# Second inversion ended in load 1 with its transpositions apart, first weight in whole rows, copies of the mixing and gram products ahead of conversion

## The chip, the core and the metric

The kernel runs on one core of a Trainium2 chip. A core has engines that run side by side, each through its own queue in order: TensorE (PE, matrix products, with PEld for its weight loads), VectorE (DVE), ScalarE (ACT), GpSimd (POOL), and SyncE (SP), which here only issues transfers (DMAs) between memory and the core. The metric is device time in microseconds from the launch's begin to its end; lower is better.

## The reference

For each of 4 batches and 8 heads (head size 48, 768 steps), a delta rule runs over the steps:

```python
k_n = k / (np.linalg.norm(k, axis=-1, keepdims=True) + 1e-06)
for t in range(S):
    y[:, :, t] = einsum(q[:, :, t], state)
    v_old = einsum(state, k_n[:, :, t])
    state = state + beta[t] * outer(k_n[:, :, t], v[:, :, t] - v_old)
```

The heads' outputs are put side by side (`x`, 768 x 384 for each batch), and a second block follows:

```python
mixed = real(fft(fft(x, axis=1), axis=2))
u = x + mixed
un = (u - mean(u)) / sqrt(var(u) + 1e-06)
out = u + maximum(un @ w_ch1, 0) @ w_ch2
```

`w_ch1` is 384 x 1536 and `w_ch2` 1536 x 384. Both arrive as 64-bit floats; all else is 32-bit.

## The kernel before, in words

**Blocks.** The recurrence is computed in loads of 128 steps: 6 loads to a batch, 24 in all, `g` is the load's number. In a load, chunks of 64 steps are turned into products: a gram matrix of the keys (`pre_a`, which copies the turned keys KT, L321, and the gram G, L380 and L386, and its masked half GU, L396), the inverse of a triangular matrix built from it, and then steps that carry the state S from chunk to chunk (`step`, with U at L721 and S at L740) and give the load's outputs (`outputs`, L763 and L773).

**Inversions.** Four loads share one inversion (`invert16`, `invert`), which runs on DVE. `invert16(1)` serves loads 4 to 7. It is a generator of 46 steps: a transposition in, 12 small operations on the norms and a scaling, then 15 pairs of a product (L518) and a sum (L521), and two transpositions of 128 x 1024 elements at the end: G (L524) and A (L526), both reading M. `pre_m16(g)` uses them: its first step copies G to Z on ACT (L609), its second makes PE's product of Z with GU, copies it to ND (L618) and copies A to MT (L625); three more products follow (L646, L648, L650), then the values are scaled (L630) and multiplied.

**Conversion.** `weight(0)` and `weight(1)` load the two weights in 12 pieces each of 384 KB and build 32-bit floats from the 64-bit words. A piece goes through ACT (L277, L282, L283) and DVE (L278, L294, L298, L300 and, one or two pieces later, the final product L290), and the next piece's load is issued behind it (L255). `convert(1)` and `advance(conv, n)` move this generator by half a piece at a time; a conversion step in the texts is two such halves. The first weight's pieces are 128 columns of all three row blocks, so a load has runs of 1 KB; the second's are one row block of all columns, runs of 3 KB. The first weight's temporary buffer takes the place of M of the inversion.

**Mixing and the two products.** `fourier(b)` gives one block of 128 rows at a time: PE's product with `dtab`, a copy Q on ACT (L874), and six operations on DVE (L883 to L891). `mlp(b)` normalizes (L912), turns (PE transpositions, copies unT at L923), makes the first product over 12 column blocks (`first_of`, its result copied as hT, L933) and the second (`second_of`). PE's results lie in pools of two buffers each: `pair`, `one` (also for the turned keys and the mixing) and `post` (the two products of the second block and its transpositions). A PE product waits until the copy that reads a buffer has been made.

**Order.** The order of PE, DVE, ACT and POOL is written out by hand in the program text, by advancing generators (`with tc.manual_schedule`). Two places differ. SP's order is always a planner's. And in loads 6 and 7 only PE's order is by hand: there a planner with its own estimates orders the other engines, and may also place their instructions among the last ones of the part before.

Loads 0 to 5 (the first batch) are a loop of their own: in each, `nm` is `pre_m16` of the next load and `n2` of the one after, `late` the outputs of the load before, c0 and c1 the two chunk steps, and `fill(n)` issues n steps of the second inversion, or, where it has ended, of the folds before the mixing. Then `fourier(0)` begins, and a loop over the 12 column blocks of the first product (`for fc in range(KF)`) issues for each block: the product and its copy hT (`side`); one conversion step; in blocks 1, 3, 6 and 9 one row block of the mixing (`f`); and one piece of `rest`, the keys of loads 9 to 11 (k1, k2, k3), the last steps of `pre_m16(7)` and the queries of load 6. The third inversion (`invert16(2)`) is issued after it, in loads 6 and 7.

Of the kernel before, what the change touches and what calls it, by code (L numbers as in the profile page):

```python
# [64 lines left out]
def kernel(  # L65
# [13 lines left out]
    DFF = moe_w_ch1.shape[1]  # L79
# [3 lines left out]
    KD = DM // 128  # L83
# [129 lines left out]
    w1 = const.tile([128, KD, DFF], F32, name="w1")  # L213
# [10 lines left out]
    def weight(last):  # L224

        if moe_w_ch1.dtype == F32:
            if last:
                nc.sync.dma_start(out=w2, in_=moe_w_ch2.rearrange("(c p) m -> p c m", p=128))  # L230
            else:
                nc.sync.dma_start(out=w1, in_=moe_w_ch1.rearrange("(c p) f -> p c f", p=128))
            return
        w1v = moe_w_ch1.bitcast(I32).rearrange("(c p) (f two) -> p c f two", p=128, two=2)
        w2v = moe_w_ch2.bitcast(I32).rearrange("(c p) (m two) -> p c m two", p=128, two=2)
        n = DM
        flat = "p e t m -> p (e t m)"
        if last:
            pieces = [(w2v[:, i:i + 1], w2[:, i:i + 1]) for i in range(KF)]

            E, O3 = spare.pop()
            ring = E.rearrange(flat).bitcast(I32).rearrange("p (i m two) -> p i m two", m=n, two=2)
            tmp = O3.rearrange(flat).rearrange("p (i e m) -> p i e m", e=2, m=n)
            tmp = [tmp[:, i] for i in range(3)]
            deep = 3
        else:
            pieces = [(w1v[:, :, i:i + 128], w1[:, :, i:i + 128]) for i in range(0, DFF, 128)]
            ring = wk.tile([128, 4, n, 2], I32, tag="big", bufs=2, name="w64")
            tmp = None
            deep = 4  # L250

        def stage(i):
            if i < len(pieces):
                src = pieces[i][0]
                nc.sync.dma_start(  # L255
                    out=ring[:, i % deep].rearrange("p (c f) two -> p c f two",
                                                    c=src.shape[1]), in_=src)

        for i in range(deep):
            stage(i)  # L260
        yield
        if tmp is None:
            tmp = [wk.tile([128, 2, n], F32, tag="M", name="wtmp0"),
                   wk.tile([128, 2, n], F32, tag="unT", bufs=2, name="wtmp1")]

        def of(i):
            t = tmp[i % len(tmp)]
            return ring[:, i % deep, :, 0], ring[:, i % deep, :, 1], t[:, 0], t[:, 1].bitcast(I32)


        lag = len(tmp) - 1
        for i in range(len(pieces) + lag):
            if i < len(pieces):
                lo, hi, man, num = of(i)


                nc.scalar.activation(man, lo.bitcast(U32), ACT.Copy, scale=2.0 ** -52, bias=1.0)  # L277
                nc.vector.tensor_scalar(num, hi, 0xFFFFF, None, op0=ALU.bitwise_and)  # L278
            if 0 < i <= len(pieces):

                num0 = of(i - 1)[3]
                nc.scalar.activation(num0, num0, ACT.Relu, scale=-1.0, bias=edges[:, 0:1])  # L282
                nc.scalar.activation(num0, num0, ACT.Relu, scale=-2.0 ** 23,  # L283
                                     bias=edges[:, 1:2])
            yield
            if i >= lag:
                _, _, man0, num0 = of(i - lag)
                dst = pieces[i - lag][1]
                c = dst.shape[1]
                nc.vector.tensor_tensor(dst, man0.rearrange("p (c f) -> p c f", c=c),  # L290
                                        num0.bitcast(F32).rearrange("p (c f) -> p c f", c=c),
                                        op=ALU.mult)
            if i < len(pieces):
                nc.vector.scalar_tensor_tensor(man, num, 2.0 ** -20, man, op0=ALU.mult,  # L294
                                               op1=ALU.add)

                man = man.bitcast(I32)
                nc.vector.scalar_tensor_tensor(man, hi, -2 ** 31, man, op0=ALU.bitwise_and,  # L298
                                               op1=ALU.bitwise_or)
                nc.vector.tensor_scalar(num, hi, 20, 0x7FF, op0=ALU.logical_shift_right,  # L300
                                        op1=ALU.bitwise_and)
                stage(i + deep)
            yield
# [7 lines left out]
    KTs, Gs, GXs, rounds, pre, xs = {}, {}, {}, {}, {}, {}  # L311
# [147 lines left out]
    def invert16(r):  # L459

        G = Gs.pop(r)
# [12 lines left out]
        A, M, Ad, Md = whole(A2), whole(M2), blocks(A2), blocks(M2)  # L474
# [38 lines left out]
        for j in range(V16 - 1):  # L513
            n = V16 - 1 - j
# [7 lines left out]
                                    op=ALU.add)  # L522
            yield
        nc.vector.transpose(G.rearrange("p m s -> p s m"), M.rearrange("p t s -> p s t"))  # L524
        yield
        nc.vector.transpose(A.rearrange("p m t -> p t m"), M)  # L526
        rounds[r] = (A, G, nT)
        yield

    LQs = {}  # L530
# [432 lines left out]
    def advance(gen, n=1):  # L963
        for _ in range(n):
            if next(gen, "end") == "end":
                return False
        return True

    def drain(gen):
        for _ in gen:  # L970
            pass
# [121 lines left out]
    with tc.manual_schedule(engines=engines):  # L1093
# [65 lines left out]
        def convert(n):  # L1159
            advance(conv, n)  # L1160

        def fill(n):

            while n > 0 and advance(inv1):
                n -= 1
            while n > 0 and advance(fd):
                n -= 1

        keys = [pre_a(g) for g in range(2 * RL, 3 * RL)]
        for g in range(NL - 1):  # L1170
            c0, c1 = step(g, 0), step(g, 1)
            nm, n2 = ms[g + 1], ms[g + 2]
            load_k(g + 2)
            load_v(g + 2)
            if g == 0:
                advance(c0)
                fill(4)
                advance(nm)
                advance(n2)
                advance(c1)  # L1180
                fill(4)
                advance(nm)
                advance(n2)
                advance(c1)
                fill(4)
                advance(nm)
                advance(n2)
                drain(nm)
                advance(n2)
                drain(qs[1])  # L1190
                advance(qs[2])
                advance(ms[3])
            else:
                advance(c0)
                fill(4)
                if g == 2:
                    drain(inv1)
                    advance(n2)
                if g > 1:
                    convert(1)  # L1200
                advance(nm)
                advance(late)
                advance(c0)
                fill(4)
                advance(n2)
                drain(late)
                if g == 4:
                    fold = folds(0)
                    fd = part(fold, 8)
                    advance(keys[0])  # L1210
                advance(nm)
                advance(c1)
                fill(3)
                if g > 1 and g != 4:
                    convert(2)
                drain(nm)
                advance(n2)
                advance(c1)
                if g == 4:
                    convert(2)  # L1220
                    advance(n2)
                    drain(qs[g + 1])
                    convert(1)
                else:
                    fill(3)
                    if g > 1:
                        convert(1)
                    advance(n2)
                    if g > 1:
                        convert(g - 1)  # L1230
                    drain(qs[g + 1])
                if g + 2 < NL:
                    advance(qs[g + 2])
                if g > 1 and g < 4:
                    advance(ms[g + 3])
            late = outputs(g)
            if g == 1:
                nc.sync.dma_start(out=evt, in_=cn["even"].ap())
                nc.sync.dma_start(out=odt, in_=cn["odd"].ap())
                nc.sync.dma_start(out=dtab, in_=cn["dtab"].ap())  # L1240
            if g == 2:
                for i in range(2 * RL, 2 * RL + 3):
                    load_c(i)
                load_q(NL)
                load_q(NL + 1)
# [44 lines left out]
        rest = [k1, ms[7], k1, ms[7], k2, ms[7], k2, k3, nq, k3]  # L1290
        for fc in range(KF):
            advance(side)
            advance(conv, 2)
            if fc in (1, 3, 6, 9):
                advance(f)
            if fc < len(rest):
                advance(rest[fc])
        drain(f)
        for m in ms[6:] + keys[1:]:
            drain(m)  # L1300
# [54 lines left out]
```

## Time and profile before

Four runs took 748.22, 752.25, 752.93 and 752.98 us: median 752.59.

| | us |
|---|---|
| median of the runs | 752.59 |
| the profiled execution | 748.22 |
| its span, first to last instruction | 746.4 |
| PE busy in the span | 690.0 |
| DVE busy | 377.5 |
| ACT busy | 264.4 |
| the two weights' products on PE (ph and po) | 208.5 and 204.7 |

Times in all lists are microseconds from the span's start. L12 is line 12 of the kernel. In a row of a timeline stand the start, the duration, the engine, the line, the operation, what it writes and reads (`out<-in`), the size, how many instructions were merged, and in brackets how long the engine stood idle before and what ended that. The granted clock is the share of TensorE's full clock that the chip let it have. `E` and `O` in conversion rows are buffers in which the second weight is converted.

In the chain of work that ended last, PE holds 74% of the span, DVE 16%, ACT 5%. The first batch's loads take the time from 40 to 113 us, the mixing begins there, the loop over column blocks runs from 131 to 167 us, and loads 6 and 7 with the third inversion from there to 203 us.

### The profile page before, as it was taken

The numbers are of one execution on the slowest core, as the hardware profiler recorded it, in microseconds if no ns is written. First come the engines' busy times: TensorE is split into PE (matmuls) and PEld (weight loads), VectorE is DVE, ScalarE is ACT, GpSimd is POOL, SyncE is SP. The second block draws the span as 40 slices with busy tenths as digits, with TensorE's granted clock in tenths as the row PEclk, the third lists the DMA queues.
The fourth block names the chain that finished last, engine by engine and source line by source line (L and its number), as shares of the span: only waits on it lengthen the run. The fifth ranks groups of instructions, "written<-read, shape, count | busy, mean of one in ns | idle before, by whom it ended". The sixth has DMA issues, their size and how long they took to land.

```text
span 746.4 us, 23081 instructions
## 1 busy us (share of the span) xinstructions
PE 690.0 (92%) x10176; PEld 529.5 (71%) x10176; DVE 377.5 (51%) x957; ACT 264.4 (35%) x644; POOL 78.7 (11%) x138
## 2 busy tenths in 40 slices
PE   7877878797999978999999999999999999999998
PEld 4676767675767656878768778878677688777684
DVE  5867877689812797261497228188312241600000
ACT  5544763787424222224322333133223121311120
POOL 8000000110000012021010220030112000200000
PEclk8799999989999998999999999999999999999999
DMA  9942452053113221002222211011210000000000
GB/s 153 220 74 41 118 117 85 12 138 102 35 40 69 56 47 20 10 11 57 50 45 49 45 40 28 1 33 34 44 33 14 12 12 1 22 1 21 11 11 21
DMA packets 111863, 36.10 MB, mean 48 GB/s; under 512 B 101873, under 2 KB 109842, under 8 KB 111762
## 3 DMA queue, kind: packets, MB, share of 16 engines
q1 hardware_dynamic: 109938, 33.86, 21.2%
q8 instruction: 80, 1.31, 0.7%
q0 software_dynamic: 640, 0.43, 0.4%
q10 hardware_dynamic: 1184, 0.33, 0.3%
q14 instruction: 21, 0.17, 0.1%
HBM read 29.88 MB, written 4.72 MB: 46 GB/s over the span
## 4 chain that ended last, share of the span: by engine, by line
PE 74%; DVE 16%; ACT 5%; issue 2%; DMA 1%; POOL 0%; DVEq 0%; ACTq 0%; SPq 0%
PE po L110 24%; PE ph L110 22%; PE one L110 15%; PE pair L110 9%; PE one L113 2%; DVE M L451 1%; DVE tmp L447 1%; PE ptr L113 1%; DVE w L290 1%; PE unread L1106 1%; ACT wtmp L283 1%; DMA C<-in_k_dram 1%; ACT wtmp L282 1%; DVE M L521 1%; PE pf L110 1%
## 5 line engine op out<-in xcount | busy, mean ns | idle before, releaser
L110 PE MATMUL ph<-unT,w 128*128 128x256 f32 x864 | 208.5, 393 | 1.1 <-ACT unT L923 0.6
L110 PE MATMUL po<-w,hT 128*128 128x384 f32 x576 | 204.7, 494 | 0.0
L110 PEld LDWEIGHTS ph<-unT,w 128*128 128x128 f32 x864 | 162.8, 194 | 26.2 <-ACT hT L933 0.9
L110 PEld LDWEIGHTS po<-w,hT 128*128 128x128 f32 x576 | 103.5, 190 | 56.3
L933 ACT ACTIVATE hT<-ph 128x256 f32<-128x256 f32 x144 | 55.2, 383 | 146.7 <-PE ph L110 145.9
L946 DVE TENSOR_TENSOR x<-x,po 128x384 f32<-128x384 f32 x24 | 13.2, 551 | 107.0 <-PE po L110 107.0
L740 DVE TENSOR_TENSOR S<-S,pair 128x192 f32<-128x192 f32 x40 | 14.0, 350 | 72.2 <-PE pair L110 72.1
L110 PEld LDWEIGHTS one<-V,MT 64*64 64x64 f32 x768 | 29.0, 136 | 20.6 <-issue 8.8
L883 DVE TENSOR_TENSOR x<-x,one 128x193 f32<-128x193 f32 x24 | 8.5, 354 | 68.7 <-ACT Q L874 68.7
L110 PE MATMUL one<-V,MT 64*64 64x48 f32 x768 | 34.2, 223 | 4.7 <-DVE V L699 2.7
L451 DVE TENSOR_TENSOR M<-M,tmp 128x31 f32<-128x31 f32 (+15 forms) x93 | 34.5, 371 | 3.2
L447 DVE TENSOR_TENSOR tmp<-A,M 128x31 f32<-128x31 f32 (+15 forms) x93 | 34.1, 366 | 2.5
L699 DVE TENSOR_TENSOR V<-V,pair 128x192 f32<-128x192 f32 x33 | 11.5, 349 | 38.2 <-PE pair L110 31.4
L110 PEld LDWEIGHTS one<-dtab,F 97*128 97x128 f32 (+1 forms) x192 | 25.1, 191 | 7.3 <-ACT KT L321 2.2
L895 POOL TENSOR_SCALAR rstd<-mv 128x1 f32<-128x1 f32 x24 | 6.4, 266 | 223.2 <-DVE mv L891 223.2
L110 PE MATMUL one<-MT,ND 64*64 64x64 f32 x768 | 27.7, 219 | 0.9 <-ACT MT L648 0.7
L321 ACT ACTIVATE QT<-one 128x512 f32<-128x512 f32 x24 | 14.2, 594 | 39.5 <-PE one L113 39.4
L110 PE MATMUL one<-dtab,F 97*128 97x97 f32 (+1 forms) x192 | 26.0, 275 | 1.8 <-ACT KT L321 1.8
L110 PEld LDWEIGHTS pair<-S,KT 48*64 48x64 f32 x528 | 10.7, 133 | 22.6 <-issue 11.0
L110 PEld LDWEIGHTS one<-MT,ND 64*64 64x64 f32 x768 | 25.1, 135 | 2.3 <-ACT MT L648 0.8
L567 POOL TENSOR_TENSOR MT<-A,pack 128x512 f32<-128x512 f32 x12 | 12.7, 1055 | 130.8 <-PE one L110 65.2
L110 PEld LDWEIGHTS pair<-U,K 64*64 64x64 f32 x704 | 15.3, 133 | 15.2 <-issue 13.0
(178 smaller groups left out, 1012.1 us busy)
## 6 DMA issues: line engine op xcount, KB each, us to landing
w<-in_moe_w_ch_dram SPq DMA_DIRECT2D x12, 384.0 KB, 5.8
E<-in_moe_w_ch_dram SPq DMA_DIRECT2D x12, 384.0 KB, 3.3
out_dram<-x SPq DMA_DIRECT2D x24, 192.0 KB, 1.9
K<-in_k_dram SPq DMA_DIRECT2D x92, 48.0 KB, 2.5
V<-in_v_dram SPq DMA_DIRECT2D x92, 48.0 KB, 2.3
C<-in_k_dram SPq DMA_DIRECT2D x18, 192.0 KB, 9.2
Q<-in_q_dram SPq DMA_DIRECT2D x18, 192.0 KB, 3.4
w<-in_q_dram SPq DMA_DIRECT2D x6, 192.0 KB, 8.2
```

The source lines that it names most:

```text
L110: nc.tensor.matmul(o, lhsT=lhsT, rhs=rhs, start=start, stop=stop, skip_group_check=True)
L113: nc.tensor.matmul(o, lhsT=src, rhs=ident[0:src.shape[0], 0:src.shape[0]], is_transpose=True, start=start, stop=True, skip_group_check=True)
L282: nc.scalar.activation(num0, num0, ACT.Relu, scale=-1.0, bias=edges[:, 0:1])
L321: nc.scalar.activation(dst.rearrange("p h j t -> p (h j t)"), pt, ACT.Copy)
L447: nc.vector.tensor_tensor(t, A[:, j + 1:W, j:j + 1].broadcast_to([128, n, j + 1]), M[:, j:j + 1, 0:j + 1].broadcast_to([128, n, j + 1]), o ...
L451: nc.vector.tensor_tensor(M[:, j + 1:W, 0:j + 1], M[:, j + 1:W, 0:j + 1], t, op=ALU.add)
L567: nc.gpsimd.tensor_tensor(MT, MTd[:, m8, None, :].broadcast_to([128, 8, 2, W]), m_blk[:, None, :, None].broadcast_to([128, 8, 2, W]), op=A ...
L699: nc.vector.tensor_tensor(R4, R4, pw[:, :, 0:2 * D].rearrange("p a (j e) -> p a j e", e=D), op=ALU.subtract)
L740: nc.vector.tensor_tensor(s1v, s0.rearrange("p h j e -> p h (j e)"), pk, op=ALU.add)
L883: nc.vector.tensor_tensor(near, near, pb[:, 0, 0:MH + 1], op=ALU.add)
L933: nc.scalar.activation(hT[:, fc, :], ph, ACT.Relu)
L946: nc.vector.tensor_tensor(x[:, T, :], x[:, T, :], po, op=ALU.add)
```

## The change

In `weight`, the first weight's pieces become one row block by 384 columns. In `invert16`, the entry in `rounds` is made between the two last transpositions, so that `pre_m16` may be issued between them. In the loop over loads 0 to 4 the fills of loads 0 and 1 grow to 5, 5, 5 and 5, 5, 4, 1; in load 2 the first step of `n2` comes right after c0, without a fill, and the rest of the inversion, now only A's transposition, after c0's second half, with the first conversion half behind it. In the loop over column blocks the conversion step moves behind the mixing and `rest`.

```diff
@@ weight
-            pieces = [(w1v[:, :, i:i + 128], w1[:, :, i:i + 128]) for i in range(0, DFF, 128)]
+            pieces = [(w1v[:, c:c + 1, i:i + n], w1[:, c:c + 1, i:i + n])
+                      for i in range(0, DFF, n) for c in range(KD)]
@@ invert16
         nc.vector.transpose(G.rearrange("p m s -> p s m"), M.rearrange("p t s -> p s t"))
+        rounds[r] = (A, G, nT)
         yield
         nc.vector.transpose(A.rearrange("p m t -> p t m"), M)
-        rounds[r] = (A, G, nT)
         yield
@@ loads 0 to 4, g == 0
-                fill(4)
+                fill(5)
...
@@ loads 0 to 4, g > 0
                 advance(c0)
-                fill(4)
                 if g == 2:
-                    drain(inv1)
                     advance(n2)
-                if g > 1:
+                else:
+                    fill(5)
+                if g > 2:
                     convert(1)
                 advance(nm)
                 advance(late)
                 advance(c0)
-                fill(4)
+
+                fill(5)
+                if g == 2:
+                    convert(1)
                 advance(n2)
                 drain(late)
...
                 advance(c1)
-                fill(3)
+                fill(4 if g == 1 else 3)
...
-                    fill(3)
+                    fill(1)
@@ loop over column blocks
         for fc in range(KF):
             advance(side)
-            advance(conv, 2)
             if fc in (1, 3, 6, 9):
                 advance(f)
             if fc < len(rest):
                 advance(rest[fc])
+            advance(conv, 2)
```

More of the change, by code (lines that the diff above doesn't have):

```diff
@@ L1194 @@
                 advance(c0)
-                fill(4)
                 if g == 2:
-                    drain(inv1)
                     advance(n2)
-                if g > 1:
+                else:
+                    fill(5)
+                if g > 2:
                     convert(1)
@@ L1203 @@
                 advance(c0)
-                fill(4)
+                fill(5)
+                if g == 2:
+                    convert(1)
                 advance(n2)
```

## The prediction

> **What bounds the kernel now.** I read the page first: the span, the busy shares and the 40 slices.
>
> ```profile
> span 746.4 us, 23081 instructions
> ...
> PE 690.0 (92%) x10176; PEld 529.5 (71%) x10176; DVE 377.5 (51%) x957; ACT 264.4 (35%) x644; POOL 78.7 (11%) x138
> ...
> PE   7877878797999978999999999999999999999998
> ...
> DVE  5867877689812797261497228188312241600000
> ```
>
> PE is busy nine tenths and more from slice 11 (205 us) on, but for slices 14 and 15; before that seven or eight tenths. All that the diff touches lies before 205 us. Busy time by stage came next (columns: PE, PEld, DVE, ACT, POOL, granted clock, DMA share, GB/s).
>
> ```profile
> 131.00:167.00 36.00, 29.73 (x278) 25.14 (x279) 26.57 (x71) 27.89 (x66) 4.40 (x9) 0.86 0.30 78
> 167.00:203.00 36.00, 30.95 (x402) 23.65 (x402) 34.12 (x97) 22.55 (x52) 2.61 (x4) 1.00 0.28 70
> 203.00:746.00 543.00, 526.34 (x6807) 393.04 (x6802) 218.50 (x549) 143.96 (x368) 54.76 (x78) 0.99 0.13 29
> ```
>
> After 203 us PE idles 16.7 us of 543, so what is won or lost before 203 us moves the end one for one. From 167 to 203 us DVE is the bound (34.1 of 36 us). Then I read the timelines of each engine around the changed places.
>
> **Part 1: the second inversion (load 1 and load 2).** Before, its last loop operations and both transpositions stand at the head of load 2, and everything of that load queues behind them:
>
> ```profile
> 67.77 1.98 DVE L524 STREAM_TRANSPOSE G<-M 128x1024 f32<-128x1024 f32 x1
> 69.66 1.88 DVE L526 STREAM_TRANSPOSE A<-M 128x1024 f32<-128x1024 f32 x1
> ...
> 71.85 0.68 DVE L650 TENSOR_TENSOR MT<-Z,one 128x512 f32<-128x512 f32 x1
> ...
> 74.34 0.55 DVE L630 TENSOR_TENSOR V<-V,nT 128x384 f32<-128x384 f32 x1
> ...
> 69.78 0.91 ACT L609 ACTIVATE Z<-G,pack 128x256 f32<-128x256 f32 x2 [2.86 <-DVE G L524]
> ...
> 70.83 1.97 PE L110 MATMUL one<-Z,GU 64*64 64x64 f32 x32 [2.53 <-ACT Z L609]
> ```
>
> PE stands 2.53 us for Z, which needs G; L650 and, behind it, the value scaling L630 wait on DVE for both transpositions, though PE had L650's product at 67.5. The generator has 46 steps; 15 are issued before load 0. Before: 12 in load 0, 14 in load 1, 5 in load 2. After: 15, 15 (G's transposition is the 45th), and A's in load 2 behind both halves of step c0.
>
> Cost in load 0: three more loop operations at 0.25 to 0.3 us. The first stands ahead of Z L646 (44.84), which followed DVE's own queue: +0.25. The second falls into DVE's 1.16 us wait before 47.98: 0. The third delays L650 (49.40) to 50.0, but the next Z (50.41) waited for PE: 0 more. Load 0: +0.25.
>
> Cost in load 1: with five in place of four ahead of L650 and again ahead of L773, the latter moves from 59.36 to 59.99 (0.25, then 0.31, then 0.07 as later operations are smaller). PE's 60.49 products waited for L773 and the copy L775 behind it (1.57 us idle): +0.63 in all. The four ahead of Z L646 fall into its 1.59 us wait: 0. G's transposition (1.98) then runs at 64.75 to 66.7; LQ L556 (65.76, would be 66.39) moves to 66.65, and PE's next use of it is at 67.96: 0. If that cover were gone it would cost 0.26.
>
> Load 2 after, on DVE: U 67.44, L650 68.2 (its product comes at 68.1), S 69.05, A's transposition 69.3 to 71.2, L278, L773 71.5, L630 71.95. ACT copies Z at 67.5, so PE's Z,GU runs at 68.9. What is late next is A: L277, queued ahead of ND L618 on ACT, writes the buffer that A's transposition reads, so it waits to 71.2, ND to 71.7, MT L625 to 72.2 to 73.1; PE's products of V start at 72.6 and last 1.3, so that isn't late. Before, V's scaling was at 74.34 and those products at 74.94: 74.94 - 72.6 = 2.34 us earlier, with the +0.63 already paid. Loads 2 to 5 are otherwise unchanged (fills there find the inversion done), so **part 1: -2.35 us**. Ends: -3.0 if the half clock after the stall (granted 0.50 from 71 to 74 us) would have cost more than DVE's row; -1.2 if the six operations moved ahead in loads 0 and 1 were each paid in full (6 x 0.3 = 1.8 in place of 0.63).
>
> **Part 2: whole rows.** Twelve loads of 384 KB stay twelve; a run per row grows from 1 KB to 3 KB, 384 runs to 128. The page has both shapes: this weight lands in 5.8 us, the second, already in whole rows, in 3.3. I take 0, since in the waits of 40 to 131 us no instruction waits for a load of this weight; four are issued ahead and each later one has over 6 us. With no cover it would be 2.5 us, once. L290 writes 128x384 in 557 ns for this weight and 546 for the other: 12 x 0.01, nothing. Column group 6 to 8 of the first product needs piece 8, done in the loop's second pass, and group 9 to 11 piece 11, in its fifth: in time.
>
> The Trainium skill ("DMA: Bandwidth & Descriptors", Specifications) puts line rate at runs of 512 B and more, which both shapes pass, so by it the 2.5 us would be no gain even uncovered. The sum is the same.
>
> **Part 3: the order in the loop over 12 column blocks.** PE's own order does not change; on ACT and DVE the mixing (Q L874, adds L883 to L891) and the gram copies now precede each conversion step. A step is DVE L290, L294, L298, L300, L278 (2.07 us start to start), 0.39 to ACT L282, then 0.64 and 0.65 to the next L290: 3.2 us around. Mixing adds Q, 0.35, 1.9 of DVE: 6.0. Before:
>
> ```profile
> 146.71 0.31 ACT L874 ACTIVATE Q<-one 128x193 f32<-128x193 f32 x1
> 146.92 0.37 ACT L933 ACTIVATE hT<-ph 128x256 f32<-128x256 f32 x1
> ...
> 147.82 0.45 PE L113 MATMUL one<-pack,C 128*128 128x128 f32 x1 [4.18 <-ACT O L277]
> ```
>
> PE waited 4.18 us for a product buffer that Q and L883 free. I followed the queues with these rows (in before's times). Block 1: Q 135.72 (138.03 before), its adds end 137.96, step 1 starts there (134.94 before). Block 3: Q 145.08, L650 147.32, step 3 at 147.9 (143.45), L282 149.8. PE's transposition starts at 146.05, 1.7 us sooner. But hT of block 4 is behind step 3's L282 and L283: 151.0 (146.92), and block 6's products need its buffer: PE stands from 148.3 to 151.4 instead. Block 6: Q 156.0 (155.71), step 6 158.25 (153.09). Block 9: Q 165.84 (165.71), grams 166.06 (165.92). So mixing and grams end where they did, +0.13, and the conversion is one step behind: step 9 comes after block 9's adds, where before it was done at 163.8. The wait didn't go; it moved from the copies to hT.
>
> What that meets:
>
> ```profile
> 166.06 0.36 DVE L883 TENSOR_TENSOR x<-x,one 128x193 f32<-128x193 f32 x1 [1.86 <-ACT Q L874]
> ...
> 167.13 1.97 DVE L476 STREAM_TRANSPOSE A<-G 128x1024 f32<-128x1024 f32 x1
> ...
> 179.30 0.36 DVE L278 TENSOR_SCALAR O<-E 128x384 int32<-128x384 int32 x1 [1.10 <-DMA E<-in_moe_w_ch_dram]
> ...
> 199.49 1.94 DVE L526 STREAM_TRANSPOSE A<-M 128x1024 f32<-128x1024 f32 x1
> 201.27 0.35 DVE L740 TENSOR_TENSOR S<-S,pair 128x192 f32<-128x192 f32 x1
> ```
>
> DVE is full from 167 to 201.3 with the third inversion and the rest of the conversion, and PE waits for L740 behind it. One more step is +2.07 there, less up to 1.10 of the wait for E. hT of block 10 (ACT 167.88) now queues behind step 9's L282 and L283, to 171.2, or 173.1 if L476 comes first on DVE; PE's transpositions for the next group (168.83) wait for its buffer, 2.8 to 4.7 us, but PE later stood 2.47 for S L738 and 0.86 for V L699. So +1.0 to +3.5; I take **+1.6**, between 1.0 and 2.07 plus 0.13, since DVE's row decides and PE's delay is nearly covered. Below zero isn't excluded: if DVE fills its bubbles the part is worth up to PE's 1.7 sooner.
>
> The granted clock fell to 0.50 at 70.9 us after an idle stretch of 2.53 us, and for 146 to 152.8 us after the one of 4.18; a window at half clock is 3.4 us long in the trace, and costs up to 1.7 us where PE decides.
>
> The Trainium skill ("TensorE: Matmul & The Clock Gate", Part 1) lets the clock drop after an idle window of about 3.4 us, free-running. By that the stretches of 2.4, 3.1 and 2.4 us in the loop would mostly keep full clock, by the 2.53 us row they need not; PE doesn't decide in the loop, so the sum stays.
>
> **Sum.** -2.35 + 0 + 1.6 = -0.75 us. The profiled execution took 748.22 (span 746.4 and 1.8 around it), so 747.5 of its kind; the runs shown are 748.22, 752.25, 752.93 and 752.98, median 752.59, and three of four lie 4 us above the profiled one with nothing in the page to say why. I put the difference on the median: **751.8**. Own range, from the ends -3.0 + 1.0 and -1.2 + 3.5: 750.6 to 754.9.
>
> **Rivals.** *Loop gains too.* For: PE's 4.18 and 1.75 us waits in 143 to 162, and the half clock after them. Against: hT takes the wait over. Worth -2.35 - 1.7 - 1.7 (one half-clock window less) = -5.75: 746.8. Chance 0.35; the order of DVE and ACT from 167 us on is a planner's, not the text's, and may pack better than I laid it.
>
> *Slower: the block 10 copy hT behind step 9.* Place: ACT queue at 168 us. Price: next group's transpositions 4.7 us late, one half-clock window 1.7, DVE's step 2.07 not covered: 8.5, less 2.35: +6.1, 758.7; it decides once the loop loses over 2.35 + 3.8 = 6.1 us. Against: the 2.47 us PE stood at 178.4. Chance 0.22.
>
> *Part 1 does nothing.* G's transposition in load 1 delays LQ and U, and the stall only moves. Then +1.6 to +2.2: 754.5; against it, DVE's row has L630 2.4 us sooner. Chance 0.05. The forecast keeps 0.38.
>
> **Numbers.** Within 0.5% (3.8 us, about what a measurement of this kernel can tell from no change): 0.38 + 0.05 = 0.43; faster 0.35; slower 0.22. The range reaches to both rivals: 745.5 to 758.5.
>
> **What would show it.** G's transposition before 67 us and no 2.5 us stall of PE before Z,GU; PE's products of V some 2.3 us sooner; full clock at 71 to 74. In the loop, Q of block 3 sooner but hT of block 4 some 4 us later, and L290 one step behind. S L740 after the third inversion at 200.5 us. It is wrong if DVE is idle in that stretch, if the transpositions of the next group come over 5 us late, or if a load of the first weight is waited for.

## The result, and the profile after

The changed kernel took 753.48 us (median of 49 runs, 747.39 to 756.94), the kernel before on the same chip 751.51 (75 runs, 747.17 to 755.78). The ratio is 1.0027, with a 95% interval of 1.0015 to 1.0038: 1.1 to 2.9 us slower. Forecast were 0.75 us less; the sign was wrong, the size small both ways. Single executions of one kernel lie up to 6 us from their median. The one profiled before (748.22) was near the low end and the one after (755.35) near the high end, so their distance of 7.1 us overstates the change, and what follows compares stretches within a profile, and medians.

The page of the profile after (its span, busy times, and PE, DVE and granted clock in 40 slices):

```profile
span 753.6 us, 23083 instructions
...
PE 695.5 (92%) x10176; PEld 533.4 (71%) x10176; DVE 377.9 (50%) x957; ACT 263.7 (35%) x644; POOL 79.8 (11%) x138
...
PE   6777878886999987999999999999999999999998
...
DVE  5877777669922699252398228178411241600000
...
PEclk9798999987999998999999999999999999999999
```

DVE's work is what it was (377.9 against 377.5). PE is busy 5.5 us longer with as many instructions; the granted clock was 0.966 on the mean, 0.973 before. The same three stretches as before (columns: PE, PEld, DVE, ACT, POOL, granted clock, DMA share, GB/s):

```profile
131.00:167.00 36.00, 30.83 (x282) 25.51 (x279) 24.53 (x63) 24.22 (x58) 4.64 (x9) 0.86 0.22 60
167.00:203.00 36.00, 28.92 (x261) 22.37 (x262) 32.19 (x101) 22.54 (x53) 2.87 (x4) 0.86 0.32 85
203.00:753.00 550.00, 533.24 (x6948) 398.04 (x6944) 223.95 (x553) 147.67 (x376) 55.07 (x78) 0.99 0.13 29
```

From 167 to 203 us the granted clock fell from 1.00 to 0.86, and PE did 261 instructions there where it did 402. Lines of the changed kernel behind line 247 have a number one higher than in the kernel before, A's transposition two (L528 for L526); with part 2 out of the kernel the numbers are those of before. The second inversion's end, on DVE and PE:

```profile
66.38 2.10 DVE L525 STREAM_TRANSPOSE G<-M 128x1024 f32<-128x1024 f32 x1
...
70.93 1.95 DVE L528 STREAM_TRANSPOSE A<-M 128x1024 f32<-128x1024 f32 x1
...
73.65 0.55 DVE L631 TENSOR_TENSOR V<-V,nT 128x384 f32<-128x384 f32 x1
...
70.38 1.05 PE L110 MATMUL one<-Z,GU 64*64 64x64 f32 x29
73.79 0.33 PE L110 MATMUL pair<-MT,K 64*64 64x64 f32 x2 [1.59 <-DVE x L774]
```

The stand of 2.53 us (PE waiting) ahead of Z,GU is gone; a stand of 1.59 us comes in its place behind A's transposition, ahead of MT,K. The value scaling L631 is 0.69 us earlier in this execution. The loop, on PE, then ACT, then DVE:

```profile
147.09 1.09 PE L113 MATMUL one<-pack,C 128*128 128x128 f32 x4 [2.61 <-DVE x L885]
...
152.29 1.94 PE L110 MATMUL ph<-unT,w 128*128 128x256 f32 x6 [1.89 <-ACT hT L934]
...
176.15 0.90 PE L113 MATMUL ptr<-pack,un 128*128 128x128 f32 x3 [4.97 <-ACT hT L934]
...
174.56 0.61 ACT L283 ACTIVATE O<-O,edges 128x384 int32<-128x384 int32 x1 [0.78 <-DVE O L301]
175.21 0.62 ACT L284 ACTIVATE O<-O,edges 128x384 int32<-128x384 int32 x1
175.73 0.36 ACT L934 ACTIVATE hT<-ph 128x256 f32<-128x256 f32 x1
...
185.11 0.36 DVE L739 COPY S<-pair 128x192 f32<-128x192 f32 x1 [1.22 <-PE pair L110]
...
207.17 0.35 DVE L741 TENSOR_TENSOR S<-S,pair 128x192 f32<-128x192 f32 x1 [0.35 <-PE pair L110]
```

The turning of the keys behind block 4's products waits 2.61 us where it waited 4.18, and block 6's products wait 1.89 us for hT, as laid out (3.1 there). But block 10's copy of hT stands behind both relus (L283, L284) of a conversion step, and PE stands 4.97 us ahead of the turning of the next group. Before, PE waited 2.47 us for the copy into S; now DVE waits 1.22 us for PE there. From the loop's first product to S behind the third inversion it is 69.93 us before (131.34 to 201.27) and 74.97 after (132.20 to 207.17). This length, called **the stretch** from here on, is the measure of the loop below.

### The profile page after: what moved, and what is told of

It is laid out like the page before. It is cut to its first block, busy times and chain, and to the rows that moved or that the text cites. A ratio compares the mean times of both kernels' runs of the same rounds, so it can differ in the third digit from the quotient of the medians.

```text
span 753.6 us, 23083 instructions
## 1 busy us (share of the span) xinstructions
PE 695.5 (92%) x10176; PEld 533.4 (71%) x10176; DVE 377.9 (50%) x957; ACT 263.7 (35%) x644; POOL 79.8 (11%) x138
## 4 chain that ended last, share of the span: by engine, by line
PE 76%; DVE 14%; ACT 6%; issue 2%; DMA 0%; DVEq 0%; ACTq 0%
PE po L110 24%; PE ph L110 23%; PE one L110 15%; PE pair L110 9%; PE one L113 2%; PE unread L1107 2%; DVE M L452 1%; DVE tmp L448 1%; PE ptr L113 1%; ACT wtmp L284 1%; ACT wtmp L283 1%; PE pf L110 1%; DVE A L407 1%; DVE G L456 1%; DVE A L477 1%
## 5 line engine op out<-in xcount | busy, mean ns | idle before, releaser
L110 PEld LDWEIGHTS one<-V,MT 64*64 64x64 f32 x768 | 31.4, 145 | 18.5 <-issue 8.6
L110 PE MATMUL one<-V,MT 64*64 64x48 f32 x768 | 36.7, 231 | 2.2 <-issue 1.0
```

The source lines that it names most:

```text
L110: nc.tensor.matmul(o, lhsT=lhsT, rhs=rhs, start=start, stop=stop, skip_group_check=True)
```

## The experiments

Ratios are against the kernel before on the same chip, with 95% intervals; 0.1% is 0.75 us.

**The parts one by one.** Part 1 alone has the hunks in `invert16` and in loads 0 to 4, part 2 alone the hunk in `weight`, part 3 alone the loop's:

```diff
             advance(side)
-            advance(conv, 2)
             if fc in (1, 3, 6, 9):
                 advance(f)
             if fc < len(rest):
                 advance(rest[fc])
+            advance(conv, 2)
```

> Only the second inversion's part (fills, the entry between the transpositions, load 2's order). Theory: this part is a gain, but smaller than the 2.35 us of the prediction, because a stand of PE of about 2 us in load 1 lets a half-clock window fall into the first batch in some executions: 0.5 to 2.4 us below the kernel before (ratio 0.997 to 0.999). Rival: it is this part that costs: 1 to 2.5 us above (1.001 to 1.003).

> Only the first weight in whole rows. Theory: no instruction waits for these loads, ratio 0.999 to 1.001. Rival: loads of keys and values share the queue and come earlier or later: over 1.5 us either way.

> Only the conversion step moved behind the mixing and the rest in the loop over column blocks. Theory: hT of block 10 queues on ACT behind a whole conversion step, PE's transpositions for the next group wait some 5 us for its buffer and then run at half clock: 3 to 5.5 us above the kernel before (1.004 to 1.007). Rival (the prediction's term): DVE's one step more decides, 1.0 to 2.1 us above (1.001 to 1.003).

> The change without its third part. Theory: the sum of the first two, 0.5 to 2.4 us below the kernel before (0.997 to 0.999), and so 3 to 6 us below the whole change. Rival (first part costs): 1 us or more above the kernel before.

| | median | ratio | loop's start | the stretch |
|---|---|---|---|---|
| part 1 alone | 748.18 | 0.9944 (0.9914 to 0.9974) | 128.53 | 69.20 |
| part 2 alone | 751.67 | 0.9994 (0.9967 to 1.0020) | 131.44 | 70.09 |
| part 3 alone | 755.91 | 1.0056 (1.0029 to 1.0082) | 134.83 | 73.45 |
| parts 1 and 2 | 748.03 | 0.9958 (0.9937 to 0.9978) | 132.56 | 70.45 |
| the kernel before | 752.12 | 1 | 131.34 | 69.93 |

Part 1 gains, part 2 does nothing, part 3 loses 4.2 us (2.2 to 6.2). The whole change without part 3 beats both kernels. Where the stretch grows is seen when it is cut into four pieces at three events on DVE: the third inversion's first transposition (L476), the sum into V (L699) and the inversion's last-but-one transposition (L524); the fourth piece ends at S. The kernel before, then part 3 alone:

```profile
131.34:167.13 35.79, 29.86 (x278) 25.27 (x279) 26.36 (x70) 27.71 (x66) 4.40 (x9) 0.86 0.30 78
167.13:184.60 17.47, 13.33 (x162) 10.01 (x160) 16.36 (x49) 12.51 (x29) 1.37 (x3) 1.00 0.40 109
184.60:197.51 12.91, 12.51 (x125) 9.99 (x125) 12.40 (x46) 6.54 (x15) 1.24 (x1) 1.00 0.21 41
197.51:201.27 3.76, 3.65 (x57) 2.18 (x56) 3.76 (x3) 2.00 (x4) 0.00 (x0) 1.00 0.01 4
```

```profile
134.83:170.74 35.91, 28.80 (x282) 23.80 (x282) 24.34 (x66) 25.79 (x63) 4.64 (x9) 0.90 0.27 67
170.74:190.52 19.78, 14.12 (x150) 10.73 (x149) 18.43 (x53) 13.08 (x30) 2.02 (x3) 0.74 0.43 115
190.52:204.03 13.51, 13.51 (x106) 10.54 (x106) 12.62 (x46) 6.87 (x16) 0.87 (x1) 1.00 0.22 40
204.03:208.28 4.25, 4.25 (x76) 2.86 (x79) 3.94 (x2) 2.60 (x6) 0.00 (x0) 1.00 0.01 4
```

The second piece grows by 2.31 us: DVE does 2.07 us more there (18.43 less 16.36), which is one conversion step, 6 of them in place of 5. The first piece has a step less and isn't shorter: DVE's 2.02 us of work were replaced by waiting. In the last two pieces PE is busy all of the time, 13.51 of 13.51 and 4.25 of 4.25, which it was not before: there PE sets the end. DVE's waits say the same. Before, it waited for PE nowhere from 167 us to S; with part 3 alone it does so ahead of a copy and two sums into S, 1.94 us in all:

```profile
186.23 0.36 DVE L738 COPY S<-pair 128x192 f32<-128x192 f32 x1 [1.26 <-PE pair L110]
...
196.43 0.35 DVE L740 TENSOR_TENSOR S<-S,pair 128x192 f32<-128x192 f32 x1 [0.37 <-PE pair L110]
...
208.28 0.35 DVE L740 TENSOR_TENSOR S<-S,pair 128x192 f32<-128x192 f32 x1 [0.31 <-PE pair L110]
```

PE's own account, from the transpositions of the next group to S (before, then part 3 alone):

```profile
168.83:201.27 32.44, 27.79 (x304) 20.91 (x302) 30.82 (x94) 19.90 (x44) 2.61 (x4) 1.00 0.30 76
```

```profile
177.22:208.28 31.06, 30.36 (x290) 23.16 (x294) 28.51 (x85) 18.83 (x43) 0.87 (x1) 0.87 0.31 81
```

The transpositions come 42.39 us behind the loop's start (177.22 less 134.83), before 37.49: 4.90 late. PE had 4.65 us of idle time behind them, now 0.70: 3.95 are made up. It is busy 2.57 us longer, at a clock of 0.87 in place of 1.00. Together 4.90 - 3.95 + 2.57 = 3.52, the growth of the stretch.

**Is it hT's place behind the conversion?** Three kernels take hT out from behind its block's step while the conversion stays late. The first issues steps 9 to 11 behind the loop; the second puts each block's copy of hT ahead of its conversion step, with the mixing and `rest` behind both again, so that only a lag of one step is left; the third is the second with parts 1 and 2.

```diff
 part 3, steps 9 to 11 behind the loop
-            advance(conv, 2)
+            if fc < 9:
+                advance(conv, 2)
+        advance(conv, 6)
 the order of before, one step later
             advance(side)
-            advance(conv, 2)
+            if fc:
+                advance(conv, 2)
...
                 advance(rest[fc])
+        advance(conv, 2)
```

> The third part alone, but the conversion steps of column blocks 9, 10 and 11 issued after hT of block 11. The conversion is as late as in p3_loop or later; only the last copies hT no longer queue behind it. Theory (the cost is hT of block 10): PE's stand of 4.96 us before the next group's transpositions falls below 1.5 us, no half-clock stretch of 10 us there, and the time is 2 to 4 us below p3_loop, 0 to 2.5 us above the kernel before (1.000 to 1.003). Rival (DVE's one step more decides): still 1.004 or more.

> The loop over column blocks with each hT ahead of the conversion step that it follows in p3_loop (a block: product and hT, the step of the block before, mixing, rest; the last step behind the loop). The conversion is exactly one step later than in the kernel before, as in p3_loop. Theory: without hT's wait the later conversion alone costs 0 to 1.5 us (1.000 to 1.002), and PE doesn't stand over 2 us before the transpositions. Rival: the later conversion is the cost, 1.004 or more.

> The change's first two parts with the loop of ht_first in place of its third. Theory: the two effects add, 0.993 to 0.997. Rival: 0.999 or more.

The ratios are 1.0050 (1.0029 to 1.0071), 1.0034 (1.0009 to 1.0059) and 1.0014 (0.9993 to 1.0035); the stretch is 75.18, 73.39 and 74.36 us. The wait ahead of the transpositions did go: none in the first, 0.94 us in the second. PE then stood later, 5.28 us in the first kernel (the row below), 5.36 and 5.37 in the other two:

```profile
190.67 1.09 PE L110 MATMUL one<-V,MT 64*64 64x48 f32 x16 [5.28 <-DVE V L699]
```

A stand as long came back at the sum into V, which DVE reaches one step later; in the first two kernels the second piece is 19.06 and 18.98 us, against 17.47. So hT's place isn't needed for the loss; it is only the first of two places where the late step shows. Whether it has a share, the intervals leave open (1.0034 against 1.0056). The third kernel gives back what parts 1 and 2 won: 1.0014 against their 0.9958.

**Part 1 without the larger fills.** Load 2's new order, and the entry in `rounds`, with the fills of before, so that G's transposition stays at the head of load 2:

```diff
                 advance(c0)
-                fill(4)
                 if g == 2:
-                    drain(inv1)
                     advance(n2)
-                if g > 1:
+                if g > 2:
                     convert(1)
...
                 fill(4)
+                if g == 2:
+                    convert(1)
```

> Of the first part only load 2's order: A's transposition behind both halves of c0, the fills of loads 0 and 1 as before, so that G's transposition still stands at the head of load 2. Theory: PE's stand of 2.5 us for Z stays, the values' scaling comes up to 1.9 us sooner: 0 to 1.9 us gained (0.9975 to 1.000), less than the whole first part. Rival (transpositions apart are all of the gain): 0.994 to 0.996.

The ratio is 0.9983 (0.9955 to 1.0011), so no gain is shown, and none excluded up to 3.4 us. In the profile PE's stand for Z is 2.62 us, and its products MT,K start at 74.47, as in the kernel before. Up to there the new order of load 2 alone moved nothing; what part 1 won in these rows came with G's transposition out of load 2's head.

**The half clock or the step?** Part 3 alone with 12 unread products in PE's stand, part 3 alone with every step one pass later still, and parts 1 and 2 with one step more in the loop's first pass or in pass 7:

```diff
 part 3 with unread products
         drain(nq)
+        unread = ps_one()
+        for _ in range(12):
+            nc.tensor.matmul(unread[:, 0:DM], lhsT=evt[:, 0, 0:128], rhs=evt[:, 0, 0:DM],
+                             start=True, stop=True, skip_group_check=True)
 part 3, two steps late
-            advance(conv, 2)
+            if fc:
+                advance(conv, 2)
...
+        advance(conv, 2)
         done = 3 + KF
 parts 1 and 2, a step ahead from pass 0, or from pass 7
-            advance(conv, 2)
+            advance(conv, 2 if fc else 4)
...
+            advance(conv, 4 if fc == 7 else 2)
```

> The kernel before with part 3 alone, and 12 products of 128x384 that nobody reads (some 4.3 us of PE work) put behind the gram product, where PE stood 4.96 us for hT of block 10 in the run with part 3 alone. Theory A (the conversion's place on DVE sets the end, the half clock after PE's stand is only its companion): no half-clock window at 174 us, but from the loop's first product to S after the third inversion still 72.5 to 73.5 us (73.45 with part 3 alone, 69.93 before), ratio 1.004 to 1.006. Theory B (most of part 3's loss is the 10.2 us at half clock that follows the stand): that stretch falls to 70 to 71.5 us, ratio 0.999 to 1.002.

> The kernel before with the loop's order of part 3 and every conversion step one pass later still, so two steps behind before at the loop's end. Theory A (each step that is pushed into the stretch that DVE bounds costs its DVE time, 2.07 us and more): from the loop's first product to S after the third inversion 75.5 to 77 us, ratio 1.008 to 1.011. Theory B (one long stand of PE and its half clock cost it, and a second step behind brings no second stand): 73 to 74.5 us, ratio 1.004 to 1.007.

> Parts 1 and 2 with before's loop, and one conversion step more in the first pass of the loop, so that the conversion is one step ahead. Theory A (a step's DVE time counts from 167 us on): from the loop's first product to S after the third inversion 68 to 68.7 us (69.93 before, 70.45 with parts 1 and 2), ratio 0.991 to 0.994 against 0.996 for parts 1 and 2. Theory B (before's place is where conversion, copies and loads just meet; the wait of 1.10 us for a load of E and the copies of the mixing take a step ahead back): 69.5 to 70.5 us, ratio 0.995 to 0.998.

> The same as the run with the step in the first pass, but the additional conversion step is in pass 7, behind the mixing of block 6, where DVE waited longest. Theory A: 68 to 68.7 us from the loop's first product to S after the third inversion, ratio 0.991 to 0.994. Theory B: its load of E isn't there yet, DVE waits for it ahead of the mixing of block 9, 69.5 to 71 us, ratio 0.995 to 0.999.

Ratios 1.0078 (1.0048 to 1.0109), 1.0055 (1.0028 to 1.0081), 1.0029 (1.0008 to 1.0050) and 0.9979 (0.9958 to 1.0001). The profiled executions of the first and third lasted 1352 and 3732 us, with PE busy throughout, while the other executions of these kernels took 754.87 to 759.36 and 750.38 to 755.51 us; nothing here explains these two, and they are left out. So both were profiled again, with the kernel before and part 3 alone, once each:

> Part 3 alone with 12 unread products in PE's stand, once more, for a profile. Theory A (DVE's later conversion sets the end): no half-clock window behind 174 us and still 72.5 to 74 us from the loop's first product to S after the third inversion. Theory B (half clock): 70 to 71.5 us. If the unread products come too late for the stand or a window at half clock is there all the same, the run tells nothing of the two.

> Parts 1 and 2 with the conversion one step ahead from the first pass on, once more, for a profile. It was 0.7% slower than parts 1 and 2 alone. Theory: the additional step delays the block's copies in the first passes, PE stands there over 4 us for a copy of hT or for a product buffer, so from the loop's first product to S after the third inversion 72 to 74 us. Against it: 68 to 70.5 us, and the loss lies elsewhere.

> The kernel before once more, for a second profile. Theory D (the profiled execution of before was an early one: where its half-clock windows fell spared it some 4 us that most executions pay): span 748.5 to 752, from the first product of the loop to S after the third inversion 70 to 72 us, mean clock below 0.973. Against it: span 746 to 747.5 and 69.9 us again.

> Part 3 alone once more, for a second profile. If the stand before the transpositions of the next group and the half clock behind it are the price of part 3, both are there again: a stand of 4.5 to 5.5 us, and 73 to 75.5 us from the loop's first product to S after the third inversion. If the first profile caught a mishap: a stand under 3 us and 70 to 71.5 us.

*The measure holds.* The kernel before took 753.05 us, with the loop's start at 134.33 and not 131.34, but the stretch was 70.12 again; part 3 alone had 73.77 and a stand of 4.98. The executions differ ahead of the loop: from 66 to 80 us the granted clock of the kernel before was 0.88 in the first profile and 0.64 in the second. The slower executions of the kernel before, which the prediction left unexplained, can lose time there. So the loop's start of a single profile doesn't show a gain or a loss of 3 us; the loop's loss is steady.

*Unread products.* They took 8.01 us, not 4.3. The clock stayed at 1.00 behind the loop, and the stretch was 75.39:

```profile
169.30:189.46 20.16, 18.06 (x173) 12.91 (x172) 20.14 (x61) 14.37 (x33) 2.02 (x3) 1.00 0.40 114
189.46:200.38 10.92, 10.92 (x93) 8.88 (x93) 10.41 (x37) 5.28 (x13) 0.83 (x1) 1.00 0.16 29
200.38:207.31 6.93, 6.93 (x87) 4.57 (x89) 4.19 (x4) 3.26 (x8) 0.00 (x0) 1.00 0.15 31
```

In the last piece PE, delayed by the unread products, was waited for (DVE stood 2.74 us ahead of S). DVE itself had ended the inversion 72.65 us behind the loop's start, against 70.09 before; of that 1.59 us came from the first piece, ahead of the added products, where DVE waited for a load of E. From the third inversion's first transposition to the end of its last, the kernel before, part 3 alone and this one:

```profile
167.13:201.43 34.30, 29.48 (x342) 22.18 (x340) 32.68 (x95) 21.05 (x48) 2.61 (x4) 1.00 0.28 71
```

```profile
170.74:207.97 37.23, 31.57 (x305) 23.82 (x305) 34.99 (x99) 22.27 (x51) 2.89 (x4) 0.86 0.31 76
```

```profile
169.30:204.57 35.27, 33.17 (x308) 24.83 (x307) 34.73 (x99) 20.83 (x48) 2.85 (x4) 1.00 0.31 80
```

DVE's row is 2.93 us longer than before with part 3 alone. Here, at full clock, it is 0.97 longer, with nearly the same work on DVE (34.99 and 34.73 us); the prediction's 2.07 less 1.10 is 0.97 as well. That points to PE's slow work as the larger part, with about one us left for the step. It isn't shown: this is one profile, and the added products changed SP's order of loads and DVE's order (a sum into V stands behind G's transposition). The division between step and clock stays open.

*Two steps late.* The stretch grew to 77.34 in the profile, somewhat over theory A's 75.5 to 77, but the median is part 3's (755.95 and 755.91). Theory A's price for a further step isn't shown by the times: with both intervals at some 2 us to each side, the second step's price lies between about -3 and +3 us.

*A step ahead.* Both gave no gain over parts 1 and 2 (0.9958), so theory A falls in that direction. For pass 7, pieces one to three of the stretch:

```profile
132.41:170.29 37.88, 29.42 (x278) 24.78 (x279) 28.39 (x76) 29.41 (x69) 4.41 (x9) 0.91 0.31 84
170.29:187.05 16.76, 14.68 (x162) 11.25 (x160) 16.13 (x47) 11.93 (x29) 1.32 (x3) 0.90 0.33 90
187.05:198.91 11.86, 11.46 (x94) 9.00 (x95) 11.21 (x41) 4.88 (x12) 0.83 (x1) 1.00 0.24 45
```

The first piece grew by 2.09 us, as much as the step has work, though DVE stood idle for 9.4 of its 35.79 us without it (35.79 in the kernel before and with parts 1 and 2). The next two are 1.20 and 1.07 us shorter than with parts 1 and 2 (17.96 and 12.93), the last 0.56 longer. In pass 0 it was worse: 40.48 us for the first piece, the stretch 74.46, without the single stand of over 4 us that the expectation had (PE's longest was 3.16).

## Why the prediction was wrong

**Part 1** was forecast at -2.35. Alone it measured -4.2 us (-6.5 to -2.0), which holds the forecast, but is more than the 0.5 to 2.4 us expected ahead of that run. Its rows agree with the forecast: in the profile of part 1 alone G's transposition stood at 64.60, A's at 69.14, and PE's first products behind both came 2.47 us sooner, where 2.34 was worked out:

```profile
72.00 0.33 PE L110 MATMUL pair<-MT,K 64*64 64x64 f32 x2 [1.19 <-DVE x L773]
```

Before, that row was at 74.47. Full clock at 71 to 74 us was there in this profile and in the changed kernel's. But in the changed kernel's the granted clock had fallen earlier, to 0.79 from 58 to 66 us, where it was 1.00 with part 1 alone: G's transposition comes at 66.38, 1.78 us later than at 64.60, and so the changed kernel's trace shows 0.69 of the 2.47. What makes the median gain larger than the rows is not shown; a candidate is the half clock behind the old stand, which was longer in the second profile of the kernel before (0.64 from 66 to 80 us). "Part 1 does nothing" falls.

**Part 2** was forecast at nothing, and none was found: 0.9994 (0.9967 to 1.0020), and the stretch is 70.09 us. With whole rows the weight's loads still landed in 5.8 us with part 2 alone (5.6 in the changed kernel), so the 3.3 us of the second weight don't come from its longer runs, and the prediction's 2.5 us for the uncovered case had no ground.

**Part 3** was forecast at +1.6 and cost +4.2 (2.2 to 6.2); with -2.35 and 0 this term alone turns the sign. Three statements in it:

- "The wait didn't go; it moved from the copies to hT" was right, with its places: block 6 (1.89 us), then block 10.
- "+2.07 there, less up to 1.10 of the wait for E" was right: 2.07 us more on DVE in the second piece, and with part 3 alone DVE waits for no load of E from 170 us on. (In the changed kernel it waits 1.69 us for one earlier, at 166.32, still in the loop; its first piece is 1.58 us longer than with part 3 alone.) Waits for PE came in its place.
- "DVE's row decides and PE's delay is nearly covered" is **the step that failed**, and with it "PE doesn't decide in the loop, so the sum stays". PE's delay (4.7 was put down, 4.90 measured) met 3.95 us of idle time, more than the 2.47 and 0.86 listed. But behind its stand PE worked at a granted clock of 0.87 and was 2.57 us busier, a cost that the sum put at nothing; it had 0.70 us of idle time left up to S, and DVE stood 1.94 us for it. DVE's late step and PE's late, slower work end together, where the text let one of them decide. How much each of the two would cost alone stays open.

The profile's 3.52 us is the +3.5 at which the prediction ended its span for this part, a figure that it set down without working it out; that it fits is luck. Of the signs that were named, the step's lag came, G's transposition stood before 67 us (66.38) and the stand ahead of Z,GU went. S stood at 207.17 and not at 200.5, and the turning of the next group came 43.95 us behind the loop's first product, 37.49 before: 6.46 us late, over the 5 that were to show the prediction wrong.

Of the **rivals**, "Loop gains too" falls: the granted clock in the first piece was 0.90 and 0.95 in the two profiles of part 3 alone, 0.86 and 0.90 in those before, but in the second piece 0.74 against 1.00, and there was no gain. The slower one had place and mechanism right for the kernel as changed (block 10's copy behind step 9, a stand of 4.97 us, the clock halved) and the size wrong: it added 4.7, 1.7 and 2.07, though DVE's step and PE's delay run at the same time. Worked out as above it is 3.5, not 8.5, and the 6.1 us at which it was to decide weren't reached. Its mechanism is also not the root, as the kernels with hT ahead show: by their profiles a step that is late costs as much through V.

The parts needn't add: -4.2, -0.5 and +4.2 give -0.5, and +2.0 (1.1 to 2.9) was measured. The three intervals are each some 2 us wide to both sides, which is enough for it; in the changed kernel's profile the stretch is 4.52 us longer than with parts 1 and 2 (74.97 against 70.45).

## What to carry to other kernels

Idle time inside a chain of queues needn't be room: here DVE stood 9.4 us of 35.8, yet one step more of 2 us made that stretch 2.1 us longer, and one step less didn't shorten it. When a wait is moved, follow both engines to the place where they next meet, and price the delayed engine's work at the clock that it may have after its stand. Before a wait is called the cause, take it away and see whether the stand comes back elsewhere.

## What the runs showed of the hardware

A stand's length alone doesn't settle whether the clock falls. In load 1 PE stood 1.97 us ahead of MT,K with part 1 alone and 1.98 with parts 1 and 2, at the same place (from 58 to 66 us, first the one, then the other):

```profile
58.00:66.00 8.00, 5.31 (x231) 5.09 (x223) 6.13 (x17) 3.10 (x7) 0.00 (x0) 1.00 0.26 47
```

```profile
58.00:66.00 8.00, 6.03 (x193) 5.79 (x187) 4.69 (x17) 3.21 (x7) 0.00 (x0) 0.79 0.23 42
```

The one kept full clock, the other was granted 0.79. What decided between them isn't shown. The Trainium skill ("TensorE: Matmul & The Clock Gate", Part 1) has a free-running window of about 3.4 us, which would make it a matter of when the stand comes. The same page has the clock drop after an idle window of that length; here a stand of 1.98 us came with the fall. Stands of 5.0 to 5.4 us in the loop and behind it came with one in all seven profiles that have them (part 3 twice, two steps late, hT ahead with and without parts 1 and 2, steps 9 to 11 behind the loop, the changed kernel): a granted clock of 0.74 to 0.80 in the piece of the stretch in which the stand ends.
